# Float64 weight pieces loaded one stage earlier, and the convolution taps loaded from ScalarE's queue, in a fused attention, expert and convolution kernel

## The chip, the cores and the metric

The kernel runs on one core of a Trainium2 chip. The metric is the device time of one execution in microseconds (us). Before the change the median of 3 runs is 373.08 us (371.57 to 373.48).

## The reference

Three blocks follow each other. The first is causal linear attention with a decay for each head, over batch 2, 8 heads, 768 positions and head dimension 64. The second sends each of the 1536 tokens to one of 8 experts (512 to 1024 to 512, with a ReLU between). The third is a gated convolution.

```python
# experts: e is the token's expert, p its softmax over the 8 experts
h = np.maximum(x[b, s] @ w1[e], 0.0)
out[b, s] = p[e] * (h @ w2[e])
...
# gated convolution, 5 taps
for k in range(K):
    gate_pre += conv_w[k][None, None, :] * xp[:, k:k + S, :]
gate = 1.0 / (1.0 + np.exp(-gate_pre))
return (gate * (x @ w_val) @ w_out).astype(np.float32)
```

The three weights of the last block, `w_val`, `w_out` and the taps `conv_w`, arrive as float64 and are turned into float32 on the chip, from their raw 32-bit words.

## The kernel before, in words

The whole kernel is one function, `fused_kernel`, that records instructions for the five engines. For TensorE (PE), VectorE (DVE), ScalarE (ACT) and SyncE (SP) the order of the program text is the order of execution in the stages told of here; GpSimd (POOL) is ordered by the scheduler in the expert stage. Each engine works its list in order, and so does SP, which issues most DMAs: a DMA whose buffer is not free holds up all that stand behind it on SP.

**Stages.** Attention with routing runs up to about 74 us, the eight experts up to about 296 us, and the gated convolution to the end.

**One expert.** For expert e, `up` (L804 to 820) makes four blocks of the hidden layer. Each takes 24 matmuls into a PSUM tile `ph` (there are three of these), a ReLU on ACT (L818) and the low half of the result on DVE (L819, `hh`). `up(e, 3)` reuses the tile of `up(e, 0)`, so it waits for the first L819 of the expert. `down` (L822) makes the first and then the second half of the tokens, 24 matmuls of 512 columns each. Between them `x_turn(e + 1)` (L787) transposes the next expert's tokens. All products are made of high and low halves, so every weight piece of 128 x 1024 is split: the high half on ACT (L192, `whi`), the low half on DVE (L197, `wlo`). The four `w2` pieces of expert e are split between the `up` blocks, the four `w1` pieces of e + 1 around the two `down` halves.

**Pool and loads.** Raw pieces, high halves and low halves share one pool, `w4`, of 24 buffers that are handed out in turn. A load waits for the last reader of the tile that had its buffer before. `load_next(4)` (L182) issues four loads on SP; in expert e the first call brings `w2` of e + 1, the second `w1` of e + 2. Between the two calls SP also issues four stores of zeros (L918).

**Float64 pieces.** `w_val` and `w_out` come in eight pieces of 128 x 1024 words, one for each expert, in buffers of the same pool. `split64_a(n)` (L227) issues the load (L230) and then calls `from64_a` (L200): six DVE instructions (L212 to L218) and an addition on POOL (L219). `split64_b(n)` (L233) finishes the piece an expert later, after the last `up` block: DVE L223, an ACT copy L238, POOL L239. `split64_a(e + 1)` stands at the end of expert e, behind the second `load_next(4)` on SP, and on DVE behind the last two `w1` splits and ahead of the first L819 of expert e + 1. `split64_a(0)` stands behind the last `up` block of expert 0. In expert 3 the taps are loaded too (L904) and turned at once on DVE and POOL.

Of the kernel before, what the change touches and what calls it, by code (L numbers as in the profile page):

```python
# [12 lines left out]
U32 = mybir.dt.uint32  # L13
# [7 lines left out]
DM, E, FF = 512, 8, 1024  # L21
P = 128
# [20 lines left out]
def fused_kernel(ctx, tc, qkv, lam, wgl, w1, w2, wv, cw, wo, out, dbg=None):  # L43
    nc = tc.nc
# [14 lines left out]
    def w4(shape, dtype, name):  # L59
        return w4_p.tile(shape, dtype, name=name, tag="w4")  # L60
# [110 lines left out]
    for a in range(2):  # L171
        c0 = 0 if a else P
# [9 lines left out]
    def load_next(n=1):  # L182
        for _ in range(min(n, len(w_src))):
            tiles, src = w_src.pop(0)
            raw = w4([P, 1024], F32, "wraw")
            nc.sync.dma_start(raw, src)
            tiles.append([raw])
# [34 lines left out]
    def from64_b(dst, a, m):  # L222
        nc.vector.scalar_tensor_tensor(dst, m.bitcast(F32), MIN64, a.bitcast(F32), op0=ALU.is_ge, op1=MUL)  # L223

    w64_t = {}

    def split64_a(n):  # L227
        src, c0 = (wv if n < 4 else wo), (n % 4) * 512
        raw = w4([P, 1024], U32, "wraw64")
        nc.sync.dma_start(raw, src[:, c0:c0 + 512].bitcast(U32))  # L230
        w64_t[n] = from64_a(raw)

    def split64_b(n):  # L233
        dst, c0 = (wv_t if n < 4 else wo_t), (n % 4) * 512
# [14 lines left out]
    def first_lo(n, cs=slice(0, 1024)):  # L249
        split_lo(first(n), cs)  # L250
# [272 lines left out]
    with tc.manual_schedule(engines=order_a):  # L523
        warm(10)
        scores(0, 0)
        scores(0, 1)
        mask(0)
        keys(0)
        load_qk(3)
        load_qk(4)  # L530
        scores(1, 0, True)
        scores(1, 1, True)
        mix_state(0)
        mix(0, 0)
        mix(0, 1)
        mixed(0)
        mask(1)
        keys_rest(0)
        powers()
        next_state(0)  # L540
        keep_state(0)
        queries(1)
        keys(1)
        keys_rest(1)
        scores(2, 0)
        turned(0)
        for s in range(2, NT):
            g1, g2, g3 = s - 1, s - 2, s - 3
            last = s == NT - 1
            if s < NT - 3:  # L550
                load_qk(s + 3)
            if s in (2, 4, 6, 8):
                load_next()
            if s in (9, 10):
                load_next(2)
            scores(s, 1)
            logits(g2)
            choice(g2)
            if last:
                ranks(g3)  # L560
                index_factors(g3)
            mask(s)
            decay(g1)
            shift(g2)
            exponents(g2)
            token_rows(g2)
            if 0 <= g3 < ET - 1:
                softmax(g3)
            if g3 >= 0 and not last:
                ranks(g3)  # L570
                index_factors(g3)
            mix_state(g1)
            mix(g1, 0)
            mix(g1, 1)
            mixed(g1)
            if last:
                counted_rest(g3)
                indices(g3)
                early_fetch()
            next_state(g1)  # L580
            choice_turned(g2, g1)
            inverse(g2)
            queries(s)
            kept(g2)
            if 3 <= s < 11:
                first_hi((s - 3) // 2, HALF[(s - 3) % 2])
            keys(s, range(2))
            experts(g2)
            keep_state(g1)
            if not last:  # L590
                scores(s + 1, 0)
            turned(g1, (0, 1))
            experts_turned(g2)
            turned(g1, (2, 3))
            if last:
                softmax(g2)
                parts_hi(g2)
                first_hi(4, HALF[0])
            one_hots(g2)
            if last:  # L600
                first_hi(4, HALF[1])
            keys_rest(s)
            keys(s, range(2, HK))
            if s == NT - 2:
                softmax(g2)
            if s >= 4:
                first_lo((s - 4) // 2, HALF[s % 2])
            if g3 >= 0 and not last:
                counted_rest(g3)
                indices(g3)  # L610
            counted(g2)

        ge, g0, g1 = NT - 3, NT - 2, NT - 1
        logits(g0)
        choice(g0)
        shift(g0)
        exponents(g0)
        token_rows(g0)
        mix_state(g1)
        mix(g1, 0)  # L620
        mix(g1, 1)
        ranks(ge)
        places(ge)
        parts_lo(ge)
        mixed(g1)
        choice_turned(g0, g1)
        kept(g0)
        place(ge, (0,))
        first_lo(4, HALF[0])
        experts(g0)  # L630
        inverse(g0)
        parts_hi(g0)
        turned(g1, (0, 1))
        experts_turned(g0)
        turned(g1, (2, 3))
        one_hots(g0)
        counted_rest(ge)
        counted(g0)
        softmax(g0)
        load_next(4)  # L640
        first_lo(4, HALF[1])
        place(ge, (1,))
        logits(g1)
        choice(g1)
        token_rows(g1)
        ranks(g0)
        places(g0)
        early_turn(0, (0, 1))
        choice_turned(g1, NT)
        kept(g1)  # L650
        parts_hi(g1)
        experts(g1)
        parts_lo(g0)
        place(g0, (0,))
        experts_turned(g1)
        one_hots(g1)
        shift(g1)
        exponents(g1)
        early_turn(0, (2, 3))
        counted_rest(g0)  # L660
        counted(g1)
        place(g0, (1,))
        ranks(g1)
        places(g1)
        parts_lo(g1)
        early_turn(1, (0, 1, 2, 3))
        place(g1)
        inverse(g1)
        softmax(g1)
        early_split()  # L670
        index_factors(ge)
        index_factors(g0)
        index_factors(g1)
# [94 lines left out]
    cw_raw = const.tile([P, 2 * KD * 5], U32, name="cw_raw")  # L768
# [105 lines left out]
    with tc.manual_schedule(engines=ordered):  # L874
        parts_of_answers = answers()
        for e in range(E):
            hhs = []
            if 0 < e < E - 1:
                x_fetch(e + 1)
            for j in range(KF // 2):  # L880
                up(e, j, hhs)
                if e == 0 and j == 0:
                    all_indices()
                    softmax_of(0, softmax_fetch(0))
                    x_fetch(1)
                elif e == 0 and j == 1:
                    nc.sync.dma_start(ys[ZROW:ZROW + 1, :].rearrange("o (a n) -> (o a) n", a=2), zero[0:2, :])
                elif e == 1 and j == 0:

                    nc.scalar.activation(sig, warm_sb[:, 0:1], AF.Sigmoid)  # L890
                elif e == E - 1 and j == 1:
                    early_answers()
                if e > 0:
                    w2_chunk(e, j)
                elif j < 3:
                    w2_chunk(e, j + 1)
                if 2 <= e < 5 and j == 1:
                    next(parts_of_answers)
                if e == 0 and j == 3:
                    split64_a(0)  # L900
                if j == 3 and e > 0:
                    split64_b(e)
                    if e == 3:
                        nc.sync.dma_start(cw_raw, cw.bitcast(U32))  # L904
                        from64_b(cw_sb.rearrange("p k j -> p (k j)"), *from64_a(cw_raw))
            load_next(4)
            if e + 1 < E:
                w1_chunk(e + 1, 0)
            py = down(e, 0, hhs)
            if e + 1 < E:  # L910
                w1_chunk(e + 1, 1)
                x_turn(e + 1)
            down_out(e, 0, py)
            if 1 <= e < 1 + NOV:
                for t in range(2):
                    r0 = (E + e - 2) * CAP + t * P
                    for c0 in range(0, DM, 256):
                        nc.sync.dma_start(ys[r0:r0 + P, c0:c0 + 256], zero)  # L918
            if e == E - 1:
                last_parts(py)  # L920
                early_answers_turn()
            py = down(e, 1, hhs)
            load_next(4)
            if e + 1 < E:
                w1_chunk(e + 1, 2)
                w1_chunk(e + 1, 3)
                if e == 0:
                    split64_b(0)
                split64_a(e + 1)
            if e == E - 1:  # L930
                last_place(0, [early["y"][:, a, :] for a in range(2)])
            yo = down_out(e, 1, py)
            if e == E - 1:
                last_place(1, [yo])
# [320 lines left out]
```

## Time and profile before

| what | before |
| --- | --- |
| median of 3 runs | 373.08 us (371.57 to 373.48) |
| the profiled execution | 373.38 us, of which the span is 371.6 us |
| PE busy | 338.8 us (91%) |
| DVE busy | 261.2 us (70%) |
| ACT busy | 199.3 us (54%) |
| POOL busy | 68.8 us (19%) |
| mean granted TensorE clock | 0.956 |
| DMA, mean over the span | 194 GB/s |

The profile is of one execution. Busy time counts instructions that run; matmuls are pipelined, so that a busy PE is not PE at its peak. The granted clock is the share of full speed that TensorE was given. Where the views name the end of a wait, it is inferred from semaphore events.

### The profile page before, as it was taken

What the parts mean: (1) busy time and instruction counts of PE and PEld (TensorE: products, weight loads), DVE (VectorE), ACT (ScalarE), POOL (GpSimd) and SP (SyncE); (2) the same over time, 40 slices, a digit from 0 to 9 for tenths busy, and PEclk for the clock granted to TensorE, in tenths of its full rate; (3) what the DMA queues carried; (4) which work ended last, traced back from release to release, by engine and by line L of the source; (5) the groups of instructions that cost most, each with busy time, mean ns of one, the idle gap of its engine ahead of it and who ended that gap; (6) DMA issues with size and microseconds to landing.
All of it is one profiled execution on the core that took longest, in us unless ns stands there. A gap on an engine that the chain in (4) does not pass through costs nothing.

```text
span 371.6 us, 7038 instructions
## 1 busy us (share of the span) xinstructions
PE 338.8 (91%) x2682; PEld 300.7 (81%) x2682; DVE 261.2 (70%) x539; ACT 199.3 (54%) x446; POOL 68.8 (19%) x89
## 2 busy tenths in 40 slices
PE   6999999999969959959969968997999999999995
PEld 3888887898958858859868867887898897999884
DVE  4879998768568458649739618729784189989880
ACT  1697999645545533642641741642653266756641
POOL 6000001034511210310401401401151074000000
PEclk9899999999998998987998996998999999999999
DMA  7998993748917924945944954954811063111012
GB/s 226 409 368 270 347 343 147 206 168 281 363 66 234 345 100 149 370 166 154 365 161 138 311 231 127 329 225 126 242 59 58 28 180 105 58 57 58 28 58 92
DMA packets 26116, 72.00 MB, mean 194 GB/s; under 512 B 3542, under 2 KB 6876, under 8 KB 26076
## 3 DMA queue, kind: packets, MB, share of 16 engines
q1 hardware_dynamic: 21172, 59.60, 46.3%
q0 software_dynamic: 2304, 7.42, 6.6%
q10 hardware_dynamic: 2600, 4.47, 3.1%
q8 instruction: 23, 0.38, 0.4%
q14 instruction: 17, 0.14, 0.1%
HBM read 57.79 MB, written 13.68 MB: 192 GB/s over the span
## 4 chain that ended last, share of the span: by engine, by line
PE 52%; DMA 27%; DVE 13%; ACT 3%; issue 2%; SPq 1%; ACTq 0%; DVEq 0%
PE py L827 13%; PE ph L815 10%; PE po L1046 9%; DMA wraw<-in_w_val_dram 8%; DMA wraw<-in_w_out_dram 8%; PE pv L1020 7%; DMA wraw<-in_w_dram 7%; DVE wlo L197 3%; PE po L320 2%; DMA ys<-warm_sb 2%; PE ps L294 2%; DMA qk<-in_qkv_dram 2%; DVE hh L819 2%; DVE gt L1006 1%; DVE f64a L213 1%
## 5 line engine op out<-in xcount | busy, mean ns | idle before, releaser
L815 PE MATMUL ph<-xh,whi 128*128 128x240 f32 x512 | 98.0, 296 | 23.0 <-DVE hh L819 22.7
L815 PEld LDWEIGHTS ph<-xh,whi 128*128 128x128 f32 x512 | 85.9, 208 | 25.1 <-DVE hh L819 23.8
L197 DVE TENSOR_TENSOR wlo<-wraw,whi 128x1024 fp32r<-128x1024 f32 (+1 forms) x69 | 85.4, 1254 | 11.2 <-ACT whi L192 10.9
L827 PE MATMUL py<-whi,hh 128*128 128x512 f32 x256 | 84.0, 399 | 0.0
L815 PE MATMUL ph<-xh,wlo 128*128 128x240 f32 x256 | 74.9, 294 | 0.0
L192 ACT CAST whi<-wraw 128x1024 fp32r<-128x1024 f32 (+1 forms) x69 | 66.3, 980 | 4.1 <-PE py L827 1.4
L818 ACT ACTIVATE hh<-ph 128x480 fp32r<-128x480 f32 x32 | 18.3, 572 | 78.1 <-PE ph L815 74.9
L827 PEld LDWEIGHTS py<-whi,hh 128*128 128x128 f32 x256 | 48.6, 190 | 11.0
L815 PEld LDWEIGHTS ph<-xh,wlo 128*128 128x128 f32 x256 | 53.4, 208 | 0.0
L827 PE MATMUL py<-wlo,hh 128*128 128x512 f32 x128 | 50.6, 396 | 0.0
L1006 DVE SCALAR_TENSOR_TENSOR gt<-yt,cw_sb,gt 128x256 f32<-128x256 f32 x96 | 39.0, 479 | 1.1 <-ACT gt L998 1.1
L212 DVE TENSOR_SCALAR f64a<-wraw 128x512 uint32<-128x512 uint32 x8 | 3.4, 427 | 50.6 <-DMA wraw<-in_w_out_dram 25.3
L1046 PE MATMUL po<-wo_t,gh 128*128 128x512 f32 (+1 forms) x156 | 34.6, 378 | 0.3 <-ACT gh L1031 0.3
L1020 PEld LDWEIGHTS pv<-yh,wv_t 128*128 128x128 f32 x288 | 33.7, 188 | 0.6 <-ACT yh L983 0.2
L1020 PE MATMUL pv<-yh,wv_t 128*128 128x256 f32 x288 | 34.1, 278 | 0.0
L1046 PEld LDWEIGHTS po<-wo_t,gh 128*128 128x128 f32 x156 | 27.1, 188 | 6.2 <-DVE gh L1036 0.8
L827 PEld LDWEIGHTS py<-wlo,hh 128*128 128x128 f32 x128 | 24.3, 190 | 5.2
L819 DVE SCALAR_TENSOR_TENSOR hh<-ph,hh 128x480 fp32r<-128x480 f32 x32 | 20.8, 649 | 4.9 <-ACT hh L818 4.9
L219 POOL TENSOR_TENSOR f64a<-f64a,f64s 128x512 f32<-128x512 f32 (+1 forms) x9 | 11.4, 1262 | 51.4 <-DVE f64s L218 51.4
L772 POOL DMA_INDIRECT xr<-xd,idx x14 | 18.1, 1293 | 12.2 <-DVE rows L780 5.1
L834 ACT ACTIVATE yo<-py,pe 128x512 f32<-128x512 f32 x16 | 11.1, 695 | 16.4 <-PE py L827 16.4
L294 PE MATMUL ps<-qk 64*128 64x128 f32 x176 | 15.7, 297 | 0.1
(176 smaller groups left out, 466.5 us busy)
## 6 DMA issues: line engine op xcount, KB each, us to landing
wraw<-in_w_dram SPq DMA_DIRECT2D x64, 512.0 KB, 6.7
qk<-in_qkv_dram SPq DMA_DIRECT2D x23, 512.0 KB, 7.4
ys<-yo ACTq DMA_DIRECT2D x16, 256.0 KB, 6.4
ys<-warm_sb SPq DMA_DIRECT2D x24, 128.0 KB, 6.8
xd<-xtok SPq DMA_DIRECT2D x11, 260.0 KB, 4.4
out_dram<-oo SPq DMA_DIRECT2D x11, 256.0 KB, 2.0
wraw<-in_w_val_dram SPq DMA_DIRECT2D x4, 512.0 KB, 9.4
wraw<-in_w_out_dram SPq DMA_DIRECT2D x4, 512.0 KB, 9.7
```

Of the source, the lines that this page charges most:

```text
L192: nc.scalar.copy(w[1][:, cs], w[0][:, cs])
L197: nc.vector.tensor_tensor(w[2][:, cs], w[0][:, cs], w[1][:, cs].bitcast(F32), op=SUB)
L219: nc.gpsimd.tensor_tensor(a.bitcast(F32), a.bitcast(F32), s.bitcast(F32), op=ADD)
L294: nc.tensor.matmul(ps_t[g][rh][:, hp, :], t[r, half, 256 + c0:256 + c0 + P], t[r, half, c0:c0 + P], start=True, stop=True)
L772: nc.gpsimd.indirect_dma_start(xr[:, t, :], None, xd, bass.IndirectOffsetOnAxis(ap=idx[:, 2 * e + t:2 * e + t + 1], axis=0))
L815: nc.tensor.matmul(ph[:, fi, :], w1_t[e][k][1 + a][:, f * P:(f + 1) * P], xh[b][:, k].rearrange("p t n -> p (t n)")[:, 0:C1], start=first, ...
L818: nc.scalar.activation(hh[:, 0, :, 0:C1], ph, AF.Relu)
L819: nc.vector.scalar_tensor_tensor(hh[:, 1, :, 0:C1], ph, 0.0, hh[:, 0, :, 0:C1].bitcast(F32), op0=ALU.max, op1=SUB)
L827: nc.tensor.matmul(py, hhs[f // 2][:, a, f % 2, t * P:(t + 1) * P], w2_t[e][f // 2][1 + b][:, (f % 2) * DM:(f % 2 + 1) * DM], start=(n == ...
L1006: nc.vector.scalar_tensor_tensor(gt[:, k, :], yt[:, b, k, c0 + j:c0 + j + 256], cw_sb[:, k, j:j + 1], gt[:, k, :], op0=MUL, op1=ADD)
L1020: nc.tensor.matmul(pv[:, mi, :], wv_t[:, a, k * DM + m * P:k * DM + (m + 1) * P], yh[:, b, k, :], start=first, stop=last)
L1046: nc.tensor.matmul(po, gh[:, a, k, t * P:(t + 1) * P], wo_t[:, b, k * DM + cs.start:k * DM + cs.stop], start=(i == 0), stop=(i == 11))
```

## The change

A new `load64(n)` issues the load of float64 piece n; `split64_a(n)` only turns it. `load64(0)` moves to the end of the routing stage, behind the loads of `w1` of expert 1. `load64(e + 1)` stands in expert e behind the four `up` blocks, ahead of the first `load_next(4)`. The load of the taps moves from SP's queue to ACT's.

```diff
+    def load64(n):
+        src, c0 = (wv if n < 4 else wo), (n % 4) * 512
+        w64_t[n] = w4([P, 1024], U32, "wraw64")
+        nc.sync.dma_start(w64_t[n], src[:, c0:c0 + 512].bitcast(U32))
+
     def split64_a(n):
-        src, c0 = (wv if n < 4 else wo), (n % 4) * 512
-        raw = w4([P, 1024], U32, "wraw64")
-        nc.sync.dma_start(raw, src[:, c0:c0 + 512].bitcast(U32))
-        w64_t[n] = from64_a(raw)
+        w64_t[n] = from64_a(w64_t[n])
...
         load_next(4)
+        load64(0)
         first_lo(4, HALF[1])
...
                     if e == 3:
-                        nc.sync.dma_start(cw_raw, cw.bitcast(U32))
+                        nc.scalar.dma_start(cw_raw, cw.bitcast(U32))
                         from64_b(cw_sb.rearrange("p k j -> p (k j)"), *from64_a(cw_raw))
+            if e + 1 < E:
+                load64(e + 1)
             load_next(4)
```

SP, the end of the loads issued in expert 3, before (the names in brackets are the semaphores waited for; the DMAHW ones count earlier DMAs).

```order
L186 DMA wraw<-in_w_dram 128x1024 [waits DMAHW0_49,PE_49]
L186 DMA wraw<-in_w_dram 128x1024 [waits DMAHW2_49,PE_49]
L186 DMA wraw<-in_w_dram 128x1024 [waits DMAHW3_49,PE_49]
L186 DMA wraw<-in_w_dram 128x1024 [waits DMAHW4_49,DVE_49]
L230 DMA wraw_2540<-in_w_out_dram 128x1024 [waits DMAHW5_49,PE_49]
```

The four loads of `w1` of expert 5 stand ahead of float64 piece 4. The piece takes the buffer of a high half and waits for PE: for the twelfth of the 24 products of the second `down` half.

SP again, the start of the loads issued in expert 3, now.

```order
L230 DMA wraw_2434<-in_w_out_dram 128x1024 [waits DMAHW7_49,DVE_49]
L186 DMA wraw<-in_w_dram 128x1024 [waits DMAHW2_49,DMAHW0_49,DVE_49]
L186 DMA wraw<-in_w_dram 128x1024 [waits DMAHW2_49,DVE_49]
L186 DMA wraw<-in_w_dram 128x1024 [waits DMAHW3_49,PE_49]
L186 DMA wraw<-in_w_dram 128x1024 [waits DMAHW4_49,PE_49]
```

Float64 piece 4 stands ahead of the four `w2` loads of expert 4. It waits for DVE: for the split of the expert's first `w2` piece (L197). Each `w2` and `w1` load takes the buffer one place further on in the pool's turn than before.

ACT at the end of expert 3's `up` blocks, now.

```order
L192 CAST whi<-wraw 128x1024
L240 CAST wv_t<-f64w 128x512
L907 DMA cw_raw<-in_conv_w_dram 128x40
L192 CAST whi<-wraw 128x1024 x2
L796 CAST xh<-px 128x4x128 x2
```

The taps' load stands behind the copy that closes the float64 piece (CAST wv_t) and ahead of the next expert's weight casts. Before, this list had no DMA here.

POOL at the same place, before (xr is the gather of the next tokens, pe their softmax).

```order
L239 TENSOR_TENSOR wv_t<-f64w,wv_t 128x512
L219 TENSOR_TENSOR f64a<-f64a,f64s 128x20
L772 DMA xr<-xd,idx 128x520 x2
L801 COPY pe<-xr 128x2
L219 TENSOR_TENSOR f64a<-f64a,f64s 128x512
```

The addition for the taps (128x20) stands ahead of both gathers. POOL at that place now:

```order
L241 TENSOR_TENSOR wv_t<-f64w,wv_t 128x512
L775 DMA xr<-xd,idx 128x520
L219 TENSOR_TENSOR f64a<-f64a,f64s 128x20
L775 DMA xr<-xd,idx 128x520
L804 COPY pe<-xr 128x2
```

One of the two gathers, which waits for PE's transposes in `x_turn(4)`, has moved ahead of the taps' addition. DVE's and PE's lists hold the same instructions in the same order as before.

## Rows read from the trace of the kernel before

**Rows 1.** The page's chain that ended last, shares of the span by line.

```profile
PE py L827 13%; PE ph L815 10%; PE po L1046 9%; DMA wraw<-in_w_val_dram 8%; DMA wraw<-in_w_out_dram 8%; PE pv L1020 7%; DMA wraw<-in_w_dram 7%; DVE wlo L197 3%; PE po L320 2%; DMA ys<-warm_sb 2%; PE ps L294 2%; DMA qk<-in_qkv_dram 2%; DVE hh L819 2%; DVE gt L1006 1%; DVE f64a L213 1%
```

**Rows 2.** Waits over the span: who waited for whom, us in total, times, longest.

```profile
DVE f64a L212 <- DMA wraw<-in_w_out_dram: 25.3, 4, 8.8
DVE f64a L212 <- DMA wraw<-in_w_val_dram: 25.3, 4, 9.1
...
PE ph L815 <- DVE hh L819: 22.7, 6, 5.0
```

**Rows 3.** The chain in order of time around expert 7's start: start us, us, what.

```profile
252.72 4.41 PE ph L815 x24
257.13 5.76 PE py L827 x24
262.89 0.64 PE px L792 x8
263.53 5.67 PE py L827 x24
269.20 10.75 PE ph L815 x96
```

**Rows 4.** Windows, L815 alone: the `up` blocks of experts 1 to 7, length, PE, PEld, clock.

```profile
97.34:113.28 15.94, 12.29 (x96) 12.02 (x95) 0.92 0.48 183
...
183.94:199.64 15.70, 12.64 (x96) 12.41 (x95) 0.89 0.49 168
211.55:230.06 18.51, 13.50 (x96) 13.23 (x95) 0.82 0.52 194
241.95:256.93 14.98, 12.43 (x96) 12.16 (x95) 0.90 0.42 150
269.04:279.79 10.75, 10.75 (x96) 10.71 (x95) 1.00 0.18 56
sum 110.47, PE 87.80 PEld 86.17; mean PE 12.54 PEld 12.31
```

**Rows 5.** Timeline of DVE around expert 7's start.

```profile
266.38 2.36 DVE L197 TENSOR_TENSOR wlo<-wraw,whi 128x1024 fp32r<-128x1024 f32 x2 [0.38 <-ACT whi L192]
270.32 0.43 DVE L212 TENSOR_SCALAR f64a<-wraw 128x512 uint32<-128x512 uint32 x1 [1.58 <-DMA wraw<-in_w_out_dram]
...
273.26 0.65 DVE L819 SCALAR_TENSOR_TENSOR hh<-ph,hh 128x480 fp32r<-128x480 f32 x1
```

**Rows 6.** Instructions on the pool's raw tiles: times from issue to landing, all 72 loads.

```profile
DMA to landing us min/median/max: 4.0/6.9/12.0
```

**Rows 7.** Windows of all work (PE, PEld, DVE, ACT, POOL, clock, DMA share, GB/s).

```profile
97.34:269.04 171.70, 149.04 (x914) 134.30 (x913) 110.08 (x159) 79.06 (x105) 30.32 (x30) 0.92 0.64 219
74.34:97.34 23.00, 23.00 (x158) 20.71 (x159) 18.20 (x27) 11.08 (x15) 11.73 (x12) 1.00 0.74 240
0.00:74.00 74.00, 69.67 (x951) 57.77 (x951) 59.64 (x203) 55.87 (x234) 8.28 (x31) 0.98 0.82 289
```

**Rows 8.** Timelines of DVE and ACT at the taps in expert 3.

```profile
175.63 0.18 DVE L212 TENSOR_SCALAR f64a<-cw_raw 128x20 uint32<-128x20 uint32 x1
...
178.18 2.35 DVE L197 TENSOR_TENSOR wlo<-wraw,whi 128x1024 fp32r<-128x1024 f32 x2
...
181.65 2.35 DVE L197 TENSOR_TENSOR wlo<-wraw,whi 128x1024 fp32r<-128x1024 f32 x2
...
175.63 0.62 ACT L238 CAST wv_t<-f64w 128x512 fp32r<-128x512 f32 x1 [1.89 <-DVE f64w L223]
```

**Rows 9.** DMA issues: count, KB of one, median us to landing; last, the stores L836.

```profile
ys<-yo ACTq DMA_DIRECT2D x16, 256.0 KB, 6.4
...
cw_raw<-in_conv_w_dram SPq DMA_DIRECT2D x1, 20.0 KB, 9.1
...
lam_sb<-in_lam_dram ACTq DMA_DIRECT2D x1, 6.0 KB, 4.0
...
DMA to landing us min/median/max: 2.0/6.4/7.9
```

## The prediction, made before the changed kernel ran

> **What bounds the kernel now.** I read the chain that ended last first. PE's products lead it, but 16% of the span stands on the landing of float64 pieces, on DMAs of `w_val` and `w_out` [rows 1]: a load on the path that sets the end. The waits say who suffers. DVE's first float64 instruction, L212, waited eight times, 50.6 us in all, for such a landing; PE waited six times, 22.7 us, for L819 on DVE, which stands right behind [rows 2]. So DVE stands still for a load, its next instruction is late, the three tiles `ph` fill up, and PE stops before the fourth `up` block.
>
> What that costs is read from the `up` blocks of experts 1 to 7 [rows 4]. The reader should compare the last one, expert 7, with the others: 96 matmuls in 10.75 us, PE busy all through, granted clock 1.00, against 14.98 to 18.51 us in experts 1 to 6. Two things differ. Length less busy time is idle: 2.5 us in expert 6, 5.0 in expert 5. And busy time is over 10.75: 12.43 and 13.50, at granted clocks of 0.90 and 0.82. As the two levels are 1.2 and 2.4 GHz, these are stretches at the lower level, and they come after an idle wait each time. One `up` block behind the wait in expert 6 took 4.41 us where 10.75 / 4 = 2.69 is the rule [rows 3, 4].
>
> **What is removed.** The seven windows sum to 110.47 us; seven times 10.75 is 75.25; the excess is 35.2 us [rows 4]. Of it 22.7 is the idle time [rows 2] and 12.5 the lower clock. All six waits have the float64 load as their cause, so if the piece lies in its buffer when DVE comes to L212, all 35.2 us go.
>
> Does it lie there? The load now waits for DVE's first `w2` split of expert e, right behind the first L819. In expert 7 that L819 was at 273.26, 4.2 us after the start at 269.04, with a wait ahead of it [rows 4, 5]; with 0.65 for itself and half of 2.36 for a split, the buffer is free 6.1 us into the expert. SP has nothing ahead of it by then, since the last `w1` load of the expert before went out in its second `down` half (in expert 2 SP first reads a count that DVE makes behind its second split, one block or 2.7 us later). The slowest of 72 loads took 12.0 us to land [rows 6]: 18.1. An expert without waits takes 10.75 + 5.76 + 0.64 + 5.67 = 22.8 us [rows 3], and DVE comes to L212 0.3 us before its end (266.38 + 2.36 = 268.74 against 269.04) [rows 5]. Some 4 us are left even with the slowest landing, which covers expert 2 too.
>
> Is DVE then early enough? From L212 to the first L819 it took 2.9 us [rows 5], so L819 could start 2.6 us into the next expert. PE needs it at the fourth block, 3 x 2.69 = 8.1 us in. Expert 7 is the test in the trace: there DVE still waited 1.58 us for its piece, and PE lost nothing [rows 4, 5].
>
> **What is moved.** Every `w2` and `w1` load goes out behind the float64 load and takes the next buffer of the pool. The first `w2` load now waits for the second split, some 8.8 us into the expert; its data are cast at 8.4 us into the next at the latest (10.75 less 2.3 for cast and split, before `down` reads them). That leaves 22.8 + 8.4 - 8.8 = 22.4 us, against 12.0 for the slowest landing: nothing. The last `w1` split on DVE now waits for the seventeenth product of the second `down` half (263.53 + 17 x 5.67 / 24 = 267.55) where it waited for the eleventh; it started at 266.38 + 1.18 = 267.56 anyway, and PE needs it at the twelfth matmul of the expert, at 270.3 [rows 3, 5]: nothing, with a microsecond to spare. `load64(0)` and `load64(1)` stand ahead of loads that expert 1 needs more than 10 us later: nothing. SP issues as many DMAs as before less one.
>
> **What is added: a wait for the taps.** Before, the taps were issued 20 us ahead of their use. Now ACT issues them behind the copy L238, which waits for DVE's L223, and DVE's very next instruction is L212 on the taps. In the trace that copy started at 175.63, as did L212 [rows 8]; with 0.62 for the copy the load goes out at 176.25. I call its landing time L. DVE then stands 0.62 + L longer, about L + 0.7 with the handoffs. Queued behind it are the four `w1` splits and two token splits for expert 4; the last pair ended at 181.65 + 2.35 = 184.0 [rows 8]. PE starts expert 4 at 183.94 and needs the last of them 11 x 0.112 = 1.2 us later [rows 4]. So PE is late by L + 0.7 + 184.0 - 185.1, or L - 0.4. The gather that has moved ahead of the taps' addition on POOL waits for transposes that PE makes before L is over, and adds nothing.
>
> No row shows L on this queue at this place. Bounds from the nearest rows: 2.0 us, the fastest of ACT's stores L836; 9.1 us, the taps' own load on SP behind four weight loads [rows 9]. I take 4.0, the one small load that ACT issued, `lam_sb`, since it is nearest in size and queue; the median of ACT's stores, 6.4, had thirteen times the bytes [rows 9]. PE is then 3.6 us late, and as the idle stretch is about as long as expert 6's, I add the 12.43 - 10.75 = 1.7 us that expert 6 lost to the lower clock: 5.3 us. At 2.0 it is 1.6 without a loss of clock; at 9.1 it is 8.7 + 2.8 (expert 5's 13.50 - 10.75) = 11.5 us. A rule stands against the middle value. In the Trainium skill, page "DMA: Bandwidth & Descriptors", section "Issuing engines are not separate DMA queues", it is said that DMAs of several issuing engines run on the same 16 DMA engines and interleave, so that another issuer saves only sequencer time. By that alone the taps would land no sooner from ACT than from SP, L would be 9.1, and the sum below would be 349.7; the section "Queues, rings and completion order" of the same page says that a DMA engine takes turns between queues packet by packet, which lets a small load past. No run here yet shows which holds.
>
> **The sum.** The profiled execution took 373.4 us, 1.8 more than its span and 0.3 more than the median shown. 373.4 - 35.2 + 5.3 = **343.5 us**; with the bounds of L, 339.8 to 349.7.
>
> **Rivals.**
>
> *Transfers pace the experts.* Between 97.34 and 269.04 the DMAs moved 219 GB/s x 171.7 us / 6 = 6.27 MB for each expert, with the DMA engines 0.64 busy [rows 7]. In 22.8 us that is 275 GB/s and 0.80. If the 240 GB/s of expert 0 [rows 7] were the most, an expert would take 26.1 us, 3.3 more, and six of them 20; the taps would hide in that: 373.4 - 35.2 + 20 = 358 us. Against it: the stage before ran at 289 GB/s over 74 us [rows 7].
>
> *The piece comes no sooner.* If something that I do not see holds the load until the second `down` half, as now, DVE waits as before: 373 us. For it: the load has a wait for a buffer in either place. Against it: the reader it waits for is done 16 us earlier.
>
> *The weights come late (slower).* Six experts' loads now squeeze into 35 us less, and all of them stand behind the float64 piece on one queue. If the first `w2` piece takes longer than 22.4 us to land, PE waits at the first product of `down`, at each of six boundaries. It decides the sign where the loss per boundary passes 35.2 / 6 = 5.9 us: 3.1 idle and 2.8 of clock, at a landing of 25.5 us. At 28 us it would be (5.6 + 2.8) x 6 = 50 more: 389 us. Against it: 12.0 is the slowest landing in the trace [rows 6].
>
> **How the numbers follow.** My forecast 0.74, transfers that pace 0.12, no sooner 0.04, weights late 0.04, and 0.06 for some other wait that gives back part, between 350 and 371. The range must leave out no more than 2 in 10: from 339 (all but nothing for the taps) to 354, which takes in the bounds of L and the smaller cases of pacing and of other waits. About 0.5%, 1.9 us, is what a measurement of this kernel can tell from no change. Faster by more: 0.74 + 0.12 + 0.06 = 0.92; within it: 0.04; slower: 0.04.
>
> **What would show it.** L212's waits for `w_val` and `w_out` gone from the list; the `up` windows of experts 1 to 3 and 5 to 7 at 10.8 us and clock 1.00; one new wait of DVE's L212 for the taps, 3 to 7 us, and one stretch at the lower clock in expert 4; more GB/s between experts 1 and 6. I am wrong if the expert stage still shows waits of PE at each boundary, whoever ends them, or if the taps' wait leaves PE untouched.

## The result, and the profile after

| | before | changed |
| --- | --- | --- |
| median | 373.07 us (371.57 to 373.48, 4 runs) | 342.87 us (342.02 to 344.37, 4 runs) |
| ratio to before, 95% interval | | 0.9201 [0.9158, 0.9245] |
| the profiled execution, its span | 373.38, 371.6 us | 342.29, 340.6 us |
| mean granted clock | 0.956 | 0.995 |

The forecast was 343.5 us. A ratio leaves out executions more than 1.5% above the fastest of their kernel, while medians and ranges hold them all; the profiled executions of the third and the ninth kernel below are among those left out.

From the page of the changed kernel: busy times, then the chain that ended last by engine and by line. Line numbers have grown by 2 to 5: L815 is L818 now, L819 is L822, L827 is L830, L918 is L923.

```profile
PE 327.1 (96%) x2682; PEld 289.4 (85%) x2682; DVE 257.8 (76%) x539; ACT 199.7 (59%) x446; POOL 64.6 (19%) x89
...
PE 77%; DMA 10%; DVE 6%; ACT 3%; issue 1%; POOL 1%; ACTq 0%; DVEq 0%; POOLq 0%
PE ph L818 24%; PE py L830 21%; PE po L1051 10%; PE pv L1025 8%; DMA wraw<-in_w_dram 3%; PE po L322 2%; PE ps L296 2%; DMA qk<-in_qkv_dram 2%; DMA xr<-xd,idx 2%; DMA cw_raw<-in_conv_w_dram 2%; DVE wlo L197 1%; DVE gt L1011 1%; DMA lam_sb<-in_lam_dram 1%; PE po L314 1%; PE rt L371 1%
```

The loads of `w_val` and `w_out`, 16% of the chain of before [rows 1], are gone from it; the taps' load has come in with 2%. The waits over the span (who waited for whom, us, times, longest) say the same:

```profile
DVE f64a L212 <- DMA cw_raw<-in_conv_w_dram: 6.0, 1, 6.0
...
PE ph L818 <- DVE xh L797: 2.5, 1, 2.5
...
PE ph L818 <- DVE wlo L197: 0.5, 1, 0.5
```

Of 50.6 us that L212 waited for float64 pieces nothing is left, nor of PE's 22.7 us [rows 2]. The windows of the `up` blocks of experts 1 to 7, with L818 alone, as in [rows 4]:

```profile
96.83:107.60 10.77, 10.77 (x96) 10.72 (x95) 1.00 0.68 250
...
142.25:153.05 10.80, 10.80 (x96) 10.72 (x95) 1.00 0.93 348
164.90:181.04 16.14, 13.03 (x96) 12.34 (x95) 0.89 0.59 207
...
215.59:226.35 10.76, 10.76 (x96) 10.72 (x95) 1.00 0.86 274
238.24:249.00 10.76, 10.76 (x96) 10.72 (x95) 1.00 0.25 75
sum 80.81, PE 77.69 PEld 76.67; mean PE 11.10 PEld 10.95
```

Six of seven stand at 10.8 us and 1.00, as expert 7 alone did before; expert 4 holds the taps' wait, 5.4 us. From the first `up` block of expert 0 to the end of expert 7 it is 191.20 us (73.52 to 264.72) where it was 221.18 (74.34 to 295.52): 30.0 of the 31.0 us by which the span fell. The other microsecond lies in the stages around it.

The taps in expert 3 of the changed kernel, first on DVE and ACT, then on PE (as in [rows 8]):

```profile
156.61 0.62 ACT L240 CAST wv_t<-f64w 128x512 fp32r<-128x512 f32 x1 [1.89 <-DVE f64w L223]
156.61 0.34 ACTq L907 DMA_DIRECT2D cw_raw<-in_conv_w_dram  x1
...
162.59 0.18 DVE L212 TENSOR_SCALAR f64a<-cw_raw 128x20 uint32<-128x20 uint32 x1 [6.02 <-DMA cw_raw<-in_conv_w_dram]
...
167.54 2.35 DVE L197 TENSOR_TENSOR wlo<-wraw,whi 128x1024 fp32r<-128x1024 f32 x2
...
164.90 0.27 PE L818 MATMUL ph<-xh,whi 128*128 128x240 f32 x1
167.68 0.38 PE L818 MATMUL ph<-xh,whi 128*128 128x240 f32 x1 [2.50 <-DVE xh L797]
...
169.94 0.57 PE L818 MATMUL ph<-xh,wlo 128*128 128x240 f32 x1 [0.53 <-DVE wlo L197]
```

DVE stands 6.0 us for a load of 20 KB, the `w1` splits behind it end at 167.54 + 2.35 = 169.89, and PE, which came to expert 4 at 164.90, goes on in earnest at 169.94.

### The profile page after: what moved, and what is told of

It reads as the page before. It is cut to its first block, busy times and chain, and to the rows that moved or that the text cites. A ratio compares the mean times of both kernels' runs of the same rounds, so it can differ in the third digit from the quotient of the medians.

```text
span 340.6 us, 7044 instructions
## 1 busy us (share of the span) xinstructions
PE 327.1 (96%) x2682; PEld 289.4 (85%) x2682; DVE 257.8 (76%) x539; ACT 199.7 (59%) x446; POOL 64.6 (19%) x89
## 4 chain that ended last, share of the span: by engine, by line
PE 77%; DMA 10%; DVE 6%; ACT 3%; issue 1%; POOL 1%; ACTq 0%; DVEq 0%; POOLq 0%
PE ph L818 24%; PE py L830 21%; PE po L1051 10%; PE pv L1025 8%; DMA wraw<-in_w_dram 3%; PE po L322 2%; PE ps L296 2%; DMA qk<-in_qkv_dram 2%; DMA xr<-xd,idx 2%; DMA cw_raw<-in_conv_w_dram 2%; DVE wlo L197 1%; DVE gt L1011 1%; DMA lam_sb<-in_lam_dram 1%; PE po L314 1%; PE rt L371 1%
## 5 line engine op out<-in xcount | busy, mean ns | idle before, releaser
L197 DVE TENSOR_TENSOR wlo<-wraw,whi 128x1024 fp32r<-128x1024 f32 (+1 forms) x69 | 79.7, 1167 | 19.2 <-ACT whi L192 18.9
L818 PE MATMUL ph<-xh,whi 128*128 128x240 f32 x512 | 88.6, 278 | 2.9 <-DVE xh L797 2.5
L830 PE MATMUL py<-whi,hh 128*128 128x512 f32 x256 | 83.4, 396 | 0.0
L818 PEld LDWEIGHTS ph<-xh,whi 128*128 128x128 f32 x512 | 78.7, 191 | 4.0 <-DVE xh L797 2.8
L818 PE MATMUL ph<-xh,wlo 128*128 128x240 f32 x256 | 70.9, 278 | 0.6 <-DVE wlo L197 0.5
L830 PEld LDWEIGHTS py<-whi,hh 128*128 128x128 f32 x256 | 47.9, 187 | 11.0
L830 PE MATMUL py<-wlo,hh 128*128 128x512 f32 x128 | 50.4, 394 | 0.0
L818 PEld LDWEIGHTS ph<-xh,wlo 128*128 128x128 f32 x256 | 48.9, 191 | 1.0 <-DVE wlo L197 1.0
L822 DVE SCALAR_TENSOR_TENSOR hh<-ph,hh 128x480 fp32r<-128x480 f32 x32 | 21.0, 655 | 14.8 <-ACT hh L821 14.6
L830 PEld LDWEIGHTS py<-wlo,hh 128*128 128x128 f32 x128 | 24.0, 187 | 5.2
L775 POOL DMA_INDIRECT xr<-xd,idx x14 | 16.7, 1190 | 17.2 <-PE px L795 7.8
L990 DVE TENSOR_TENSOR yh<-pt,yh 128x512 fp32r<-128x512 f32 x12 | 7.8, 682 | 11.5 <-ACT yh L988 11.4
L276 ACT ACTIVATE kd<-qk,dm 128x64 f32<-128x64 f32 x40 | 11.5, 343 | 6.7 <-DMA qk<-in_qkv_dram 6.7
```

The lines of the kernel that those rows point to most:

```text
L197: nc.vector.tensor_tensor(w[2][:, cs], w[0][:, cs], w[1][:, cs].bitcast(F32), op=SUB)
L276: nc.scalar.activation(kd[:, h, :], qk_t[g, 1][:, 0, h * D:(h + 1) * D], AF.Copy, scale=dm[:, h, P - 1:P])
L775: nc.gpsimd.indirect_dma_start(xr[:, t, :], None, xd, bass.IndirectOffsetOnAxis(ap=idx[:, 2 * e + t:2 * e + t + 1], axis=0))
L818: nc.tensor.matmul(ph[:, fi, :], w1_t[e][k][1 + a][:, f * P:(f + 1) * P], xh[b][:, k].rearrange("p t n -> p (t n)")[:, 0:C1], start=first, ...
L822: nc.vector.scalar_tensor_tensor(hh[:, 1, :, 0:C1], ph, 0.0, hh[:, 0, :, 0:C1].bitcast(F32), op0=ALU.max, op1=SUB)
L830: nc.tensor.matmul(py, hhs[f // 2][:, a, f % 2, t * P:(t + 1) * P], w2_t[e][f // 2][1 + b][:, (f % 2) * DM:(f % 2 + 1) * DM], start=(n == ...
```

## The experiments

The kernel before ran beside each group of four kernels, with medians of 375.12, 375.81 and 376.88 us; the ratios go by those. In the diffs, - and + stand against the kernel named, and ... marks lines that are left out.

**1 and 2. The taps' wait alone.** Against the changed kernel: the taps back on SP at the same place (first diff), or on ACT but in expert 1 (second).

```diff
                     if e == 3:
-                        nc.scalar.dma_start(cw_raw, cw.bitcast(U32))
+                        nc.sync.dma_start(cw_raw, cw.bitcast(U32))
```

```diff
                     nc.scalar.activation(sig, warm_sb[:, 0:1], AF.Sigmoid)
+                    nc.scalar.dma_start(cw_raw, cw.bitcast(U32))
...
                     if e == 3:
-                        nc.scalar.dma_start(cw_raw, cw.bitcast(U32))
```

> The change with its second part undone: the taps go out on SP again, at the same place of the program, where SP stands well ahead of their use. My theory (the earlier float64 pieces are the whole gain, and the taps' new wait takes 5.4 us back: 3.1 idle and 2.3 of lower clock in expert 4): 342.9 - 5.4 = 337.5 us, between 336.5 and 338.5; no wait of DVE's L212 for the taps; the up block of expert 4 at 10.8 us and granted clock 1.00. Rival (the taps are late on whichever queue, since the same DMA engines carry them): 342 to 346 us, with the wait in the same place. Rival (moving the taps off SP is a part of the gain, since they no longer stand behind weight loads): slower than 344.

> The change with the taps still on ScalarE's queue, but issued in expert 1, some 50 us ahead of their use. If it is the late issue that costs 5.4 us and not the queue: 337.5 us, as with the taps on SP. If a load on ScalarE's queue costs something by itself (ACT standing still, or lanes shared with its stores): 340 or more.

Measured: 337.87 us (337.32 to 343.57), 0.9002 [0.8925, 0.9079] of before, and 337.30 us (337.05 to 342.74), 0.8984 [0.8907, 0.9060]. PE no longer waits for DVE anywhere in the experts, and each takes 22.65 us. It is the late issue, right ahead of the use, that costs 5 us, not the queue: SP issued the taps at 141.59, DVE wanted them at 156.76 and went straight on.

```profile
141.59 0.42 SPq L907 DMA_DIRECT2D cw_raw<-in_conv_w_dram  x1
...
156.76 0.18 DVE L212 TENSOR_SCALAR f64a<-cw_raw 128x20 uint32<-128x20 uint32 x1
```

Both are faster than either kernel of the change.

**3. The other half alone.** Against the kernel before: only the taps move to ACT.

```diff
-                        nc.sync.dma_start(cw_raw, cw.bitcast(U32))
+                        nc.scalar.dma_start(cw_raw, cw.bitcast(U32))
```

> The kernel before with the second part of the change alone: only the taps move to ScalarE's queue. My theory says that the taps' wait and the float64 wait overlap on DVE: PE starts expert 4 about 5.4 us late (3.1 idle, 2.3 clock), but the wait of 3.06 us at its fourth up block and the 1.9 us of lower clock behind it go, since the float64 piece still lands at the same time: +0.4 us, 372 to 376. Rival (the costs add): 378.5. Rival (the move frees SP and is a part of the gain): under 370.

Measured: 374.90 us (370.38 to 378.08, 10 runs), 0.9938 [0.9888, 0.9988]: no loss, as forecast. The profiled execution (376.10 us) shows how: two waits of DVE's L212, the second short because the first stands ahead of it, and `up` of expert 4 at 16.41 us where it was 15.70 [rows 4].

```profile
181.87 0.18 DVE L212 TENSOR_SCALAR f64a<-cw_raw 128x20 uint32<-128x20 uint32 x1 [6.30 <-DMA cw_raw<-in_conv_w_dram]
191.35 0.43 DVE L212 TENSOR_SCALAR f64a<-wraw 128x512 uint32<-128x512 uint32 x1 [2.18 <-DMA wraw<-in_w_out_dram]
...
183.19:199.60 16.41, 12.78 (x96) 12.19 (x95) 0.90 0.52 196
```

The same wait costs 5.4 us in one kernel and nothing in the other. That is the first sign that costs do not add in the kernel before. (The interval lies just under 1, a gain of 0.1 to 1.1%.)

**4 and 5. Where the load must stand, and how many.** The taps are on SP in both. In the fourth kernel the float64 load goes behind the four `w2` loads (first diff, against the first kernel); in the fifth only the pieces of experts 1 to 3 are early (second).

```diff
-            if e + 1 < E:
-                load64(e + 1)
             load_next(4)
             if e + 1 < E:
+                load64(e + 1)
                 w1_chunk(e + 1, 0)
```

```diff
-            if e + 1 < E:
+            if e < 3:
                 load64(e + 1)
             load_next(4)
...
+                if e >= 3:
+                    load64(e + 1)
                 split64_a(e + 1)
```

> The taps on SP, and the float64 load of expert e + 1 behind that expert's four weight loads and not ahead of them. It then waits for a product of the expert's fourth up block, some 10.5 us into the expert, and the piece is wanted at 22.7: 12 us are left against a landing of 4 to 8. My theory (anything that lands before the end of the expert will do): 337.5 us, the same as with the load ahead of them. Rival (the place ahead of the weight loads is what counts, since behind them the piece lands last of five): DVE's L212 waits again and the time is 345 or more.

> The taps on SP; the float64 loads of experts 1 to 3 issued early as in the change, those of experts 4 to 7 at their old place behind the four w1 loads. My theory (each boundary stands for itself and gives back its own idle time and its own lower clock): the up blocks of experts 1 to 3 take 10.8 us at granted clock 1.00, those of experts 4 to 6 keep the excess they had, 4.95 + 7.76 + 4.23 = 16.9 us, so 337.6 + 16.9 = 354.5 us, between 352 and 357. Rival (the waits only move: a queue that is behind stays behind, or the saved time is lost again at the later boundaries): 360 or more. Rival (the gain is not local, the lower clock has a cause of its own): 345 or less, or excess in experts 1 to 3.

Measured: 337.64 us (337.29 to 338.06), 0.8999 [0.8939, 0.9058]; the piece took 8.3 to 9.5 us to land (medians for `w_out` and `w_val`) and DVE did not wait. So to stand ahead of the weight loads is not what helps. The fifth: 355.69 us (354.17 to 356.61), 0.948 [0.9417, 0.9543], within the forecast, each boundary for itself:

```profile
142.33:153.09 10.76, 10.76 (x96) 10.72 (x95) 1.00 0.92 333
164.98:180.96 15.98, 12.64 (x96) 12.37 (x95) 0.89 0.47 167
192.87:211.56 18.69, 13.50 (x96) 13.23 (x95) 0.82 0.48 184
223.53:239.99 16.46, 12.62 (x96) 12.39 (x95) 0.90 0.51 167
```

Experts 4 to 6 are 15.98 + 18.69 + 16.46 - 3 x 10.75 = 18.9 us over; 16.9 had been forecast.

**6. The lower clock alone.** Against the kernel before: PE's idle time is filled with products that nobody reads, to see whether the clock then stays up and what that gives back.

```diff
+    FILL = (0, 15, 15, 15, 15, 15, 15)
...
             for j in range(KF // 2):
+                if j == 3 and 0 < e < E - 1:
+                    fill = ps_x.tile([P, 512], F32, name="fill", tag="px")
+                    for _ in range(FILL[e]):
+                        nc.tensor.matmul(fill, identr, w1_t[e][0][1][:, 0:512], start=True, stop=True)
                 up(e, j, hhs)
```

> The kernel before, with 15 more matmuls of 128 x 512 (about 3.5 us) that nobody reads, into a free PSUM tile ahead of the fourth up block of experts 1 to 6, in the place where PE stood idle for 2.5 to 5.0 us. DVE's waits are left as they are. My theory (the lower clock of 12.5 us in all comes after an idle PE, and not from anything else in those stretches): the float64 waits of L212 stay near 50 us, the blocks behind the fill run at 1.00, and the time falls by 12.5 less 1.5 that the fill is too long in experts 4 and 6: 362 to 366 us, 0.97 of the kernel before. Rival (the clock falls for another reason, such as transfers or the other engines): 374 to 378, with 0.8 to 0.9 in the blocks behind the fill.

Measured: 374.70 us (371.12 to 376.15, 10 runs), 0.997 [0.9929, 1.0011]. **My theory fell.** The clock did what it said: the fourth `up` block of six experts, in the kernel before (first and last, and the sum of six) and with the fill (the same), whose mean granted clock over the span is 0.993:

```profile
109.22:113.28 4.06, 4.06 (x24) 3.98 (x24) 0.67 0.27 71
...
252.72:256.93 4.21, 4.21 (x24) 4.13 (x24) 0.64 0.28 75
sum 27.55, PE 27.55 PEld 27.16; mean PE 4.59 PEld 4.53
```

```profile
109.95:112.74 2.79, 2.79 (x24) 2.76 (x24) 1.00 0.00 0
...
254.14:258.13 3.99, 3.99 (x24) 3.91 (x24) 0.68 0.26 74
sum 17.95, PE 17.95 PEld 17.71; mean PE 2.99 PEld 2.95
```

Those blocks gave back 9.6 us, five of the six at 1.00, and nothing was gained. PE waited again, behind the fill and, newly, in `down`:

```profile
PE ph L816 <- DVE hh L820: 8.8, 6, 2.7
PE py L828 <- DVE wlo L197: 2.3, 3, 0.9
```

So the end of each expert was set elsewhere, and PE's idle time and its slow stretches only filled the room. **The new theory is a round**, the way from one L212 on a float64 piece to the next; it was put on record below as one that PE is no part of. Of the kernel before, DVE and SP in experts 4 and 5:

```profile
191.59 0.43 DVE L212 TENSOR_SCALAR f64a<-wraw 128x512 uint32<-128x512 uint32 x1 [7.59 <-DMA wraw<-in_w_out_dram]
195.09 2.02 DVE L197 TENSOR_TENSOR wlo<-wraw,whi 128x1024 fp32r<-128x1024 f32 x1
...
197.14 5.73 SPq L186 DMA_DIRECT2D wraw<-in_w_dram  x4
202.92 3.42 SPq L918 DMA_DIRECT2D ys<-warm_sb  x4
206.44 4.50 SPq L186 DMA_DIRECT2D wraw<-in_w_dram  x4
211.03 0.40 SPq L230 DMA_DIRECT2D wraw<-in_w_out_dram  x1
...
221.15 0.43 DVE L212 TENSOR_SCALAR f64a<-wraw 128x512 uint32<-128x512 uint32 x1 [8.81 <-DMA wraw<-in_w_out_dram]
```

A piece lands at 191.59; DVE goes on, and its first `w2` split ends at 197.11. That frees the buffer for the first `w2` load, which goes out at 197.14 (the third of the four waits for the third split, which ends at 202.05); SP works through twelve DMAs and comes to the next float64 load at 211.03, and the piece is there at 221.15. The round is 5.5 + 13.9 + 10.1 = 29.6 us. While SP waits for DVE, nothing at all is transferred, and for the first 4.5 us of that time PE stands too; in the rest of the round the DMA engines are 0.75 to 0.86 busy (windows of all work: PE, PEld, DVE, ACT, POOL, clock, DMA share, GB/s):

```profile
197.10:211.00 13.90, 13.90 (x69) 11.77 (x68) 11.86 (x23) 7.58 (x10) 3.77 (x3) 0.92 0.75 225
211.00:220.30 9.30, 8.78 (x76) 8.45 (x74) 1.34 (x2) 4.19 (x7) 0.18 (x1) 1.00 0.86 342
220.30:226.60 6.30, 1.81 (x8) 1.81 (x9) 5.35 (x9) 1.02 (x2) 1.27 (x1) 0.73 0.00 1
```

So a round is a pause and then the transfers of one expert, behind one another. How much of the 13.9 us is SP's issuing and how much the transfers themselves is not separated by these runs: between 97 and 270 us SP also waited 11 times, 15.7 us in all, for earlier `wraw` loads of its own to land.

From the first to the sixth L212 on a piece there are five rounds: (249.08 - 105.58) / 5 = 28.7 us. PE needs 22.65. The chain that ended last goes the way just told in three of the five, those of experts 1, 2 and 4. In the rounds of experts 3 and 5 it goes from L819 through PE instead; expert 3, in order of time:

```profile
166.76 5.43 PE ph L815 x24
172.19 5.60 PE py L827 x24
177.79 0.64 PE px L792 x8
178.43 2.65 PE py L827 x11
...
181.72 9.77 DMA wraw<-in_w_out_dram
```

There PE's late `up` block and its `down` products free the buffers that the last loads of the round wait for. So the round has a second arm, through PE, and the two are nearly equally long: the rounds of experts 1, 2 and 4 took 28.8, 28.7 and 29.6 us, those of experts 3 and 5 28.5 and 27.9. "No part" is too strong; what the runs can show is whether the round gets shorter when PE's arm does.

**7. Do transfers pace the experts?** Against the first kernel: one more load of 512 KB for each expert, ahead of its `w2` loads.

```diff
                 load64(e + 1)
+                nc.sync.dma_start(spare, (wv if e < 3 else wo)[:, 0:512].bitcast(U32))
             load_next(4)
```

> The taps on SP, and behind each early float64 load one more load of 512 KB on SP into a tile that nobody reads, ahead of the four w2 loads: 6.8 MB for each expert where 6.3 were, and one transfer more that the w2 pieces stand behind. My theory (PE sets the pace and the loads have slack): 337 to 340 us, no new wait of PE. Rival (the transfers are close to setting the pace, the 0.81 share of the DMA engines is their limit): 1.5 to 2 us more for each of seven experts, 346 or more, with PE or ACT waiting for wraw.

Measured: 337.87 us (337.55 to 344.62), 0.901 [0.8942, 0.9077]: free, at 301 GB/s and a DMA share of 0.85.

```profile
97.00:233.00 136.00, 136.00 (x914) 122.40 (x913) 110.72 (x160) 79.55 (x105) 33.97 (x30) 1.00 0.85 301
```

**8. The buffer or the place.** Against the kernel before: the float64 pieces in a buffer of their own.

```diff
-        raw = w4([P, 1024], U32, "wraw64")
+        w4([P, 1024], U32, "wraw64")
+        raw = f64_p.tile([P, 1024], U32, name="raw64", tag="raw64")
```

> The kernel before, but the float64 pieces have a buffer of their own, so that the load at the old place waits for no product of the second down half; the pool keeps its turn. It tells which of two things made the piece late: the buffer, or the place behind four w1 loads on SP. The trace of before had SP reach the load at about the time when the buffer came free (at 181.72 where the twelfth product ended near 181.1), so my theory is that the place alone would have kept it late: 371 to 376 us, with L212's waits still over 40 us. Rival (the buffer made it late): 337 to 350.

Measured: 373.46 us (370.99 to 376.16, 10 runs), 0.9996 [0.9931, 1.0062], with 49.5 us of waiting at L212. Freed of that wait alone, the load came no sooner: the round stayed at 28.7 us.

**9 to 12. The round itself.** The ninth is the eighth with the four stores of zeros behind the float64 load:

```diff
-            if 1 <= e < 1 + NOV:
-                for t in range(2):
...
                 split64_a(e + 1)
+            if 1 <= e < 1 + NOV:
+                for t in range(2):
...
```

The tenth is the kernel before with one more load of 512 KB ahead of the float64 load:

```diff
+                nc.sync.dma_start(spare, (wv if e < 3 else wo)[:, 0:512].bitcast(U32))
                 split64_a(e + 1)
```

The eleventh is the kernel before without the third product in `down` of experts 1 to 5, and so leaves out part of the second layer:

```diff
         for f in range(KF):
-            for a, b in PASSES:
+            for a, b in PASSES[:2] if 1 <= e <= 5 else PASSES:
...
```

The twelfth is the first kernel with the float64 load between the stores and the `w1` loads:

```diff
-            if e + 1 < E:
-                load64(e + 1)
             load_next(4)
...
             py = down(e, 1, hhs)
+            if e + 1 < E:
+                load64(e + 1)
             load_next(4)
```

> New theory, after the fill that restored the clock and gained nothing: the kernel before went round a loop that PE is no part of. A float64 piece lands, DVE's L212 goes on, DVE splits a w2 piece, the split frees the buffer that the first w2 load waits for, SP issues four w2 loads, four stores of zeros, four w1 loads and then the next float64 load. From one L212 to the next that took 28.7 us on average (105.58 to 249.08, five rounds) where PE needs 22.65. Here the pieces have their own buffer and the four stores of zeros stand behind the float64 load and not ahead of the w1 loads: 2.0 to 3.7 us less in each round, 2.9 on average. Loop theory: about 25.8 us from one L212 to the next, 6 x 2.9 = 17 us off the kernel before: 354 to 360. Rival (PE's idle time and its lower clock are what counts, and go together once the wait falls under about 1 us): 343 to 350. Rival (the loads' own landing binds, stores or not): 370 or more.

> The kernel before with one more load of 512 KB on SP for each expert, into a tile that nobody reads, ahead of the float64 load. The same load cost nothing in the change (337.87 us with it and without). Loop theory: it lengthens each round by what a load takes on SP, 1.1 to 1.4 us, so 6 to 8 us in all: 379 to 385. Rival (SP is not in the path, the buffer is free no earlier than the twelfth product of the second down half and the load waits for that): under 376.

> The kernel before without the third product (low half of the hidden layer by high half of w2) in both down halves of experts 1 to 5: 16 matmuls of 0.236 us, 3.8 us of PE's work, less for each of the five. Loop theory (PE is no part of the loop): L212 still comes every 28 to 29 us and the time stays at 370 to 376, with more idle time of PE. Rival (my first theory: the time is PE's work plus a wait of fixed length and its clock): 5 x 3.8 = 19 us less, 352 to 357.

> The taps on SP, and the float64 load behind the four w2 loads and the four stores, ahead of the four w1 loads of the second down half. It is then earlier than before by the w1 loads alone, 4.4 to 5.6 us of SP's time, 4.8 on average. Loop theory: 28.7 - 4.8 = 23.9 us a round where PE needs 22.65, so nearly all of the gain: 338 to 348. Rival (it must stand ahead of the weight loads): 360 or more.

| kernel | time, us | ratio to before | one round, us |
| --- | --- | --- | --- |
| before | 376.88 (373.66 to 381.67) | | 28.7 |
| 6, 22 us of PE in its idle time | 374.70 | 0.997 [0.9929, 1.0011] | (250.50 - 106.31) / 5 = 28.8 |
| 8, own buffer | 373.46 | 0.9996 [0.9931, 1.0062] | (248.10 - 104.69) / 5 = 28.7 |
| 11, 19 us less of PE | 376.60 (372.27 to 380.69) | 0.9958 [0.9900, 1.0017] | (247.06 - 105.93) / 5 = 28.2 |
| 10, one load more | 387.60 (386.70 to 388.78) | 1.0299 [1.0229, 1.0369] | (257.46 - 107.22) / 5 = 30.0 |
| 9, stores behind | 362.71 (361.07 to 367.92) | 0.9613 [0.9541, 0.9685] | not read |
| 12, ahead of `w1` | 340.95 (339.77 to 341.50) | 0.9055 [0.8995, 0.9115] | (210.21 - 97.56) / 5 = 22.5 |

(The ratios of 6 and 8 go by the kernel before of their own group, 375.81 us.)

**The round sets the time.** Put 6 x 15 matmuls into PE's idle time, which shortens its slow `up` blocks by 9.6 us, or take 5 x 16 away: the time stays. On PE's arm the first `down` half fell from 5.6 to 3.8 us, and the round gave back 0.5: PE's arm alone does not hold it. With the matmuls taken away PE only waits more; window of all work from expert 1 to expert 7, and the waits:

```profile
97.00:268.00 171.00, 136.43 (x831) 120.39 (x830) 109.62 (x158) 78.21 (x105) 31.82 (x30) 0.91 0.64 220
...
PE ph L815 <- DVE hh L819: 25.7, 6, 4.8
DVE f64a L212 <- DMA wraw<-in_w_val_dram: 25.5, 4, 9.0
DVE f64a L212 <- DMA wraw<-in_w_out_dram: 22.8, 4, 8.1
```

A load that was free in the seventh kernel costs 3% in the tenth. Moving four stores, whose zeros nothing in the experts reads, wins 4% (with the buffer of the eighth kernel, which alone won nothing). And the twelfth, only the `w1` loads earlier than before, has all of the gain in the experts: PE waits for DVE nowhere there. Two of these forecasts missed on size. The ninth won 14.6 us by its ratio where 17 were expected. The tenth lost 10.7 by the medians where 6 to 8 were: of that, 8.2 are in the experts (97.39 to 277.31 against 171.70). There a round is 1.3 us longer, and most of it is the piece's own landing behind one load more, 10.7 us where it was 9.8 (means of five on the chain), not SP's issuing, as had been said. The profile also has a stop of PE of 3.6 us in the convolution with no releaser. The twelfth has one of 2.0 us there too. What they are is open.

## Why the prediction was right

**The float64 waits, 35.2 us.** Right in size, and right that the early load ends them. From [rows 4], 110.47 us for seven windows became 80.81: 29.7 less, which is 35.2 less 5.4 for the taps and 0.2 spread over the rest. But the step gave a wrong account of the sum. It split 35.2 into 22.7 idle and 12.5 of lower clock, as if each were a price. The sixth kernel took most of the 12.5 away and the eleventh 19 us of PE's work, and neither moved the end. What is real is the difference of two periods: an expert took (269.04 - 97.34) / 6 = 28.6 us where PE alone needs 22.65, so 6 x 5.97 = 35.8 us. The size came out right because PE is the bound as soon as the round is broken, not because the two parts are prices. The chain of before had the round in it: `w_val` and `w_out` with 16%, but also the weight loads with 7%, the zero stores `ys<-warm_sb` with 2%, `wlo` with 3% [rows 1]. Stores of zeros on the chain are something to stop at, and I passed over them.

**Does it lie there?** Right, with more to spare than the 4 us said. SP issued the piece of expert 7 at 221.27, 5.7 us after expert 6 began (6.1 forecast); pieces took 4.6 us to land where they took 9.4 to 9.7 (medians) behind the other loads, and DVE came for it at 237.85. Some 12 us are left.

```profile
198.63 0.33 SPq L230 DMA_DIRECT2D wraw<-in_w_out_dram  x1
...
221.27 0.33 SPq L230 DMA_DIRECT2D wraw<-in_w_out_dram  x1
```

**What is moved, nothing.** Right: no weight came late, and PE has no new wait in the experts but those of the taps, a stop of 0.3 us for a gather in expert 0 aside.

**The taps, 5.3 us.** 5.4 measured, by errors that cancel. L was 5.9, not 4.0. By the working, PE's twelfth matmul would have been L - 0.4 = 5.5 us late; it was 169.94 - 166.1 = 3.8. Two terms were off: ACT issued the load at 156.61, as its copy began and not at its end (0.6), and the splits ended 7.3 us behind L212 and not 8.4 (1.1). That 1.1 is one instruction, L218 on the taps, before and now:

```profile
176.43 1.25 DVE L218 SCALAR_TENSOR_TENSOR f64s<-cw_raw,f64s 128x20 f32<-128x20 uint32 x1
```

```profile
163.39 0.18 DVE L218 SCALAR_TENSOR_TENSOR f64s<-cw_raw,f64s 128x20 f32<-128x20 uint32 x1
```

It took 1.24 to 1.25 us in the twelve kernels in which the taps were there in time, and 0.18 in the two in which DVE waited for them. In the trace of before it ran beside POOL's L239 (176.33, 1.32 us) and ended with it; now POOL stood idle. That POOL held it is not shown by a run of its own. Of the 3.8 us, 2.50 + 0.53 = 3.0 are idle; the lower clock took 13.03 - 10.77 = 2.3 (1.7 forecast), part of it inside the 3.8.

On the rule weighed there: the taps landed 5.9 us after issue on ACT, against 9.1 from SP before. The section "Issuing engines are not separate DMA queues" of the Trainium skill's page "DMA: Bandwidth & Descriptors", read by itself as in the prediction, would have had 9.1, and did not come true in the letter; but the two loads met different traffic, and from ACT in expert 1 it was 4.8, so the runs here do not tell which of the two sections was at work. That an earlier place costs nothing on either queue is what the first two kernels showed.

**The rivals.** Transfers did not pace the changed kernel's experts: 264 GB/s and a share of 0.78 (97 to 238), and a free load more at 301 and 0.85 in the seventh. The piece came sooner; no weight came late. "Some other wait" did not appear.

## What to carry to other kernels

Compare the period of one repeated instruction with the work of the busiest engine in that period. Here PE was busy for 91% and made up half of the chain (52% of the span), and the time still hardly depended on it: a load waited for a buffer, the buffer for a split, the split for an earlier load, and the issue queue tied them into a round of 28.7 us against 22.65. The Trainium skill's page "Perfetto Trace Analysis", section "Identifying the Most-Contended Engine", says to optimise the engine of highest occupancy first, and to judge TensorE's headroom by its weight loads or its share of peak work. Here the weight loads were busy for 81% of the span and the next engine for 70%; with 19 us of TensorE's work taken away, this kernel stayed at 0.9958. The same page reads repeated gaps, under "Optimization Strategy", as a possible lack of buffers; a buffer more for the float64 piece gave 0.9996 (a fourth `ph` tile was not tried). Two signs told this round from a busy engine: stretches in which the DMA engines and PE stand still together (DMA share 0.00 from 220.30, PE idle to 224.79), and idle work, such as stores of zeros, on the chain.

Break a round by moving the load that closes it ahead of things that it has no need to follow, until the round is shorter than the work: ahead of the stores alone left 362.71 us, and beyond that how far ahead matters little (337.6 and 341 us for two later places). And issue a small load long before its use: a load of 20 KB issued by the engine that precedes its user cost 5 us, and 15 us earlier nothing.

## What the runs showed that was not expected

The lower clock was not a price. After idle waits of 2.5 to 5.0 us PE's next 24 matmuls took 4.06 to 5.27 us at granted clocks of 0.50 to 0.67 (1.2 GHz for part or all of the block) where 2.79 is the time at 1.00; with matmuls in the gap they took 2.79 even behind 0.63 to 1.58 us of waiting, and 3.99 (0.68) in the one case where 2.75 us of waiting were left. Yet the time fell by no more than 0.7% [0.9929, 1.0011] for 9.6 us given back in those blocks. The clock lost behind a wait counted where PE was the bound, 2.3 us behind the taps in the changed kernel, and not in the kernel before.

One and the same load of 512 KB on SP cost nothing with the float64 load early and 10.7 us with it late. A transfer's price is its place in the round.
